# Attention and top-1 experts on one core: four wide warming products of TensorE give way to 53 small ones

## The chip, the cores and the metric

The program runs on one core of one Trainium2 chip. Its time is the device time of that core in microseconds (us); of the kernel before there are three timed runs, and one more execution was taken with the hardware profiler. Engines are named as the profile names them: PE (TensorE, its matrix products), PEld (TensorE's loads of the stationary operand), DVE (VectorE), ACT (ScalarE), POOL (GpSimd) and SP (SyncE, which here issues most of the transfers).

## The reference

Causal attention with a decay per head, in blocks, for 4 batches, 8 heads, 768 positions and 64 features, then a layer of 8 experts in which each of the 3072 tokens goes to one of them:

```python
intra = np.einsum('bhic,bhjc->bhij', qb, kb) * Dmask[None]       # Dmask = lam ** (i - j), i >= j
intra = np.einsum('bhij,bhjd->bhid', intra, vb)
inter = np.einsum('bhid,bhde->bhie', qb * lam_pow[None], kv_state)
out[:, :, sl] = intra + inter
kv_state = lam_block[None, :, None, None] * kv_state + np.einsum('bhsd,bhse->bhde', kb_dec, vb)
...
logits = x @ w_gate
expert_idx = np.argmax(logits, axis=1)
...
    h = np.maximum(xe @ w1[e], 0.0)
    out[mask] = gate_w[mask, None] * (h @ w2[e])
```

## The kernel before

The kernel has two stages. The attention stage walks over twelve steps (`order`: six blocks of 128 positions by two pairs of batches), in the loop over `i` at the end of the main function. In a step PE turns the keys and queries of the step ahead (`turn_k`, L353, into tiles `tk`; `turn_q`, L335, into `tq`), makes the routing logits of the step behind (`leave`, L480 and L485), applies the masked scores to the values (`attend_early`, L435, and `attend_late`, L443, into `op`), makes the scores of the step ahead (`score_half`, L389 and L394, into `sp`), ranks the tokens (`rank_of`, L560 and L562), applies the carried state (L421) and grows it (`grow`, L461, into `cp`). Nearly all of these are products of 64 or 128 rows by 64 or 128 columns. ACT and DVE empty the results from PSUM. SP issues the loads of queries, keys and values three steps ahead (L128), in rows of 256 bytes, and POOL issues two indirect writes per step (`send`, L541), which scatter the finished tokens to their experts' lists `xs`.

The expert stage (from about 127 us on) gathers the lists, and runs the two weight products of each expert; most of PE's time there is in L837, with 178 to 209 columns moving in each product.

The order of PE's instructions is the order in which the program is written, since the code stands in `tc.manual_schedule` for PE. All of PE's instructions, apart from a last part that runs only if an expert has too many tokens, are one straight stream without a loop.

The change is at the start. `run_up(count)` issues `count` bf16 products of a constant `ones` with itself (128 by 128 weights, 512 columns moving) into a spare bank; their results are not read. PE begins with `run_up(4)`, then `spread_lam` (L223), a product with one row, which spreads the eight decays `lam` over 128 partitions, and then a second `run_up(4)`. Behind it stand the first step's `turn_q` for its two halves (L335) with `run_up(2)` and `run_up(1)`, `turn_k` (L353) and the first scores (L389). DVE reads `spread_lam` (L225) and makes the decay tables from it.

A product of two fp32 operands is one line of the program and two pairs of instructions of PE in the trace, each a weight load and a product (L223 is one product in the program, and x2 in the trace); a transposition (L335, L353) and a bf16 product are one pair.

## Time and profile before

| | us |
|---|---|
| three timed runs: median (lowest to highest) | 441.4 (438.82 to 443.08) |
| the profiled execution: device time | 436.91 |
| its span, first to last instruction | 435.1 |
| PE busy in the span | 414.0 (95%) |
| PEld busy | 388.3 (89%) |
| DVE busy | 297.3 (68%) |
| ACT busy | 143.2 (33%) |
| POOL busy | 96.3 (22%) |

PE and PEld overlap, since the next weights are loaded while a product runs. The ends of products are modelled in the trace and their starts are not, so the pitch from start to start is the sharper measure. An idle time marked "issue" is one for which the trace shows no other engine or transfer that PE waited for.

### The profile page before, as it was taken

Reading aid. Unit: us, or ns where it says so; the run is one execution under the profiler, and the core shown is the slowest. Engines: PE = TensorE matmul, PEld = TensorE weight load, DVE = VectorE, ACT = ScalarE, POOL = GpSimd, SP = SyncE. Lnnn points to the kernel's source line nnn. Section 1 sums busy time; section 2 is a strip of 40 time slices with the busy share of each in tenths; the row PEclk is TensorE's granted clock in tenths of the full one; section 3 lists DMA queues with packets and bytes.
Section 4 is the critical chain, followed back from the end, with each engine's and each line's share of the span. In section 5 each row is a group of like instructions: output and inputs, shape, how many; then the busy total and the mean of one; then the engine's idle time right before and its main releaser. Section 6 shows DMA issues by size and latency. Waiting matters only on the chain.

```text
span 435.1 us, 11634 instructions
## 1 busy us (share of the span) xinstructions
PE 414.0 (95%) x4721; PEld 388.3 (89%) x4721; DVE 297.3 (68%) x692; ACT 143.2 (33%) x301; POOL 96.3 (22%) x123
## 2 busy tenths in 40 slices
PE   8988888999989999999999999999999999999993
PEld 5887777898878899999999999999999999999672
DVE  6777776588756876767669577766967867775601
ACT  3544344344432121330252135025214313403420
POOL 7545444441142210010011003001100200300502
PEclk9999999899999999999999999999999999999997
DMA  9988999899971499695399179638917946605201
GB/s 211 212 207 228 241 240 228 203 262 241 235 297 52 129 333 383 144 342 143 84 303 298 24 176 328 196 82 271 327 42 210 350 97 167 241 2 144 63 28 56
DMA packets 124784, 85.05 MB, mean 195 GB/s; under 512 B 83830, under 2 KB 106118, under 8 KB 124722
## 3 DMA queue, kind: packets, MB, share of 16 engines
q1 hardware_dynamic: 118720, 70.21, 59.5%
q0 software_dynamic: 4432, 13.61, 8.5%
q8 instruction: 39, 0.64, 0.6%
q10 hardware_dynamic: 1570, 0.39, 0.4%
q14 instruction: 23, 0.19, 0.1%
HBM read 65.10 MB, written 19.42 MB: 194 GB/s over the span
## 4 chain that ended last, share of the span: by engine, by line
PE 94%; issue 3%; DVE 1%; ACT 1%; POOLq 0%; POOL 0%; ACTq 0%
PE p L837 55%; PE p L945 6%; PE ph L724 5%; PE op L443 3%; PE cp L461 3%; PE op L421 3%; PE tk L353 3%; PE sp L389 3%; PE tq L335 3%; PE tx L480 2%; PE po L894 2%; PE logits L485 2%; PE op L435 2%; PE po L989 2%; PE sp L394 1%
## 5 line engine op out<-in xcount | busy, mean ns | idle before, releaser
L689 POOL DMA_INDIRECT out_dram<-o,ids x13 | 12.9, 989 | 171.0 <-ACT o L936 168.9
L837 PE MATMUL p<-hT,w2t 128*128 128x209 f32 (+5 forms) x288 | 49.4, 327 | 0.0
L837 PEld LDWEIGHTS p<-hT,w2t 128*128 128x128 f32 x288 | 47.7, 189 | 0.0
L765 ACT COPY u_qsT<-p 128x418 f32<-128x418 f32 (+6 forms) x40 | 19.2, 480 | 78.0 <-PE p L837 76.7
L541 POOL DMA_INDIRECT xs<-x,row x24 | 23.8, 991 | 74.8 <-ACT xT L451 31.7
L837 PE MATMUL p<-xgT,w1t 128*128 128x209 f32 (+6 forms) x224 | 38.7, 326 | 0.0
L837 PEld LDWEIGHTS p<-xgT,w1t 128*128 128x128 f32 x224 | 36.7, 190 | 0.0
L862 ACT ACTIVATE hT<-hT 128x418 f32<-128x418 f32 (+6 forms) x42 | 22.0, 525 | 32.5 <-DVE hT L861 32.5
L404 DVE TENSOR_TENSOR mt<-sp,tables 128x384 f32<-128x384 f32 x48 | 24.2, 549 | 7.8 <-PE sp L394 7.7
L451 ACT COPY xT<-op 128x512 f32<-128x512 f32 x24 | 12.9, 589 | 39.2 <-PE op L421 38.2
L861 DVE TENSOR_TENSOR hT<-p,u_qsT 128x418 f32<-128x418 f32 (+6 forms) x28 | 15.6, 558 | 11.9 <-ACT u_qsT L765 9.2
L724 PE MATMUL ph<-xgT,w1t 128*128 128x256 f32 (+1 forms) x128 | 21.9, 329 | 0.0
L750 DVE TENSOR_TENSOR u_qsT<-p,u_qsT 128x418 f32<-128x418 f32 (+6 forms) x20 | 11.2, 559 | 15.7 <-PE p L837 15.7
L913 DVE STREAM_TRANSPOSE yb<-yT 128x896 f32<-128x896 f32 (+2 forms) x14 | 13.6, 975 | 11.4 <-ACT yT L880 9.0
L724 PEld LDWEIGHTS ph<-xgT,w1t 128*128 128x128 f32 x128 | 19.2, 190 | 1.8 <-DVE gates_0a L634 0.2
L837 PE MATMUL p<-t_xT,s_q 128*128 128x209 f32 (+6 forms) x112 | 20.6, 326 | 0.0
L837 PE MATMUL p<-t_kd,w1t 128*128 128x209 f32 (+6 forms) x112 | 20.5, 326 | 0.0
L837 PE MATMUL p<-t_sd,w1t 128*128 128x209 f32 (+6 forms) x112 | 20.5, 326 | 0.0
L837 PE MATMUL p<-xgT,s_v 128*128 128x209 f32 (+6 forms) x112 | 20.5, 326 | 0.0
L837 PE MATMUL p<-xgT,s_k 128*128 128x209 f32 (+6 forms) x112 | 20.5, 326 | 0.0
L345 DVE TENSOR_TENSOR qsT<-tq,qdec 128x512 f32<-128x512 f32 x20 | 12.9, 685 | 9.4 <-ACT qT L341 9.4
L355 ACT COPY kT<-tk 128x512 f32<-128x512 f32 x24 | 14.3, 606 | 13.6 <-PE tk L353 13.5
(247 smaller groups left out, 920.3 us busy)
## 6 DMA issues: line engine op xcount, KB each, us to landing
w1t<-in_moe_w_dram SPq DMA_DIRECT2D x7, 2048.0 KB, 9.0
w2t<-in_moe_w_dram SPq DMA_DIRECT2D x7, 2048.0 KB, 9.8
qkv_in<-in_q_dram SPq DMA_DIRECT2D x12, 256.0 KB
q_in<-in_q_dram SPq DMA_DIRECT2D x12, 256.0 KB
y<-ye SPq DMA_DIRECT2D x6, 512.0 KB, 4.2
xb<-xs SPq DMA_DIRECT2D x32, 96.0 KB, 8.8
xb<-xs SPq DMA_DIRECT2D x24, 112.0 KB, 8.4
ye<-yb SPq DMA_DIRECT2D x12, 224.0 KB, 3.2
```

Source lines behind the costliest of these rows:

```text
L335: nc.tensor.transpose(tq[:, a, b], m.q[:, u, at:at + 2], ident)
L353: nc.tensor.transpose(tk[:, a, b], m.k[:, u, at:at + 2], ident)
L355: nc.scalar.copy(kT, tk)
L404: made = nc.vector.tensor_mul(mt[:, r], m.sp[a][r], decay[:, r, a].unsqueeze(1).to_broadcast(shp))
L541: put = tc.keep_in_program_order(nc.gpsimd.indirect_dma_start(out=xs, out_offset=bass.IndirectOffsetOnAxis(ap=row, axis=0), in_=src, in_of ...
L724: nc.tensor.matmul(ph, lhsT=piece(w1t, dc, fc), rhs=m.xgT[:, dc].rearrange("p k h -> p (k h)"), start=(dc == 0), stop=(dc == DC - 1))
L765: nc.scalar.copy(dst, src)
L837: nc.tensor.matmul(p[:, i, :], lhsT=lhs_of(lhs, rhs, c, i), rhs=rhs_of(lhs, rhs, c, i), start=(first and i == 0 and c == 0), stop=(c == ch ...
L861: nc.vector.tensor_add(outs[i][k], p, u)
L862: nc.scalar.activation(outs[i][k], outs[i][k], ACT.Relu)
L913: nc.vector.transpose(m.yb[:, i * nb:(i + 1) * nb], m.yT[i].rearrange("p d (b t) -> p b d t", t=Q))
L945: nc.tensor.matmul(p, lhsT=lhs[:, fc, :], rhs=rhs[:, fc, :], start=(first and fc == 0), stop=(fc == FC // 2 - 1), skip_group_check=True)
```

## The change

The second `run_up(4)` is replaced by `pace()`. It issues 53 products of the row `one` with itself: fp32, one row, 32 columns of weights (`Q` is 32), one column moving, all into the same 32 values of the spare bank (bank 7). Nothing reads them.

```diff
+    PACE = 53
+
+    def pace():
+
+
+        spare = bank(7, [Q, 1], "pace")
+        for j in range(PACE):
+            nc.tensor.matmul(spare, lhsT=one[:, :Q], rhs=one[:, :1], start=True, stop=True)
+
     with tc.manual_schedule(engines={mybir.EngineType.PE}):
         run_up(4)
         spread_lam = bank(6, [P, H], "lam")
         nc.tensor.matmul(spread_lam, lhsT=one, rhs=lam_row, start=True, stop=True)
-        run_up(4)
+        pace()
     nc.vector.tensor_copy(lam_bc, spread_lam)
```

PE's order of before, from the product that spreads the decays (`lam`) to the first transpositions of queries (`tq`); `spare` are the products of `run_up`:

```order
L223 MATMUL lam<-lam_row,one 128x8
L217 LDWEIGHTS ones
L217 MATMUL spare<-ones 128x512
L217 LDWEIGHTS ones
L217 MATMUL spare<-ones 128x512
L217 LDWEIGHTS ones
L217 MATMUL spare<-ones 128x512
L217 LDWEIGHTS ones
L217 MATMUL spare<-ones 128x512
L335 MATMUL tq<-impulse,qkv_in 128x128 x4
```

The same place of the changed kernel, in which all lines behind the new function stand 9 further on (L344 is the L335 of before):

```order
L232 MATMUL lam<-lam_row,one 128x8
L227 MATMUL pace<-one 32x1 x53
L344 MATMUL tq<-impulse,qkv_in 128x128 x4
L217 LDWEIGHTS ones
L217 MATMUL spare<-ones 128x512
```

Four pairs of a weight load and a product, 8 instructions, have gone. 53 fp32 products have come, which at two pairs each are 212 instructions. So every later instruction of PE stands 204 places further on in PE's stream, and none changes its place against another.

The second place is the end of a step and the beginning of the next, the same in both kernels but for the numbers of the lines; here as it stands before. `cp` is the growth of the state, `tk` and `tq` the turned keys and queries of the next step:

```order
L421 MATMUL op_2182<-qsT,st 64x128
L461 MATMUL cp<-qkv_in,kd 64x64 x16
L353 MATMUL tk<-impulse,k_in 128x128 x4
L335 MATMUL tq<-impulse,q_in 128x128 x8
L353 MATMUL tk<-impulse,k_in 128x128 x4
L480 MATMUL tx_2376<-impulse,xT 128x128 x4
```

Nothing moved there against its neighbours. What differs is the count of instructions from the start of the stream to this place, by 204. On the other engines the order is unchanged.

## Rows read from the trace of the kernel before

**Rows 1.** The page: busy time, share of the span and instructions of each engine
```profile
PE 414.0 (95%) x4721; PEld 388.3 (89%) x4721; DVE 297.3 (68%) x692; ACT 143.2 (33%) x301; POOL 96.3 (22%) x123
```

**Rows 2.** The page: the chain that ended last, by engine
```profile
PE 94%; issue 3%; DVE 1%; ACT 1%; POOLq 0%; POOL 0%; ACTq 0%
```

**Rows 3.** PE's waits in the whole span: total us, times, longest us
```profile
PE op L443 <- issue: 6.0, 5, 2.0
PE cp L461 <- issue: 2.8, 5, 1.1
PE op L421 <- issue: 1.5, 1, 1.5
...
PE op L421 <- DVE mt L404: 0.8, 1, 0.8
```

**Rows 4.** PE in order of time: start, length, products, idle before
```profile
105.42 1.15 PE L443 MATMUL op<-mt,v_in 128*64 128x64 f32 x32
106.50 0.67 PE L389 MATMUL sp<-qT,kT 64*64 64x128 f32 x16
```

**Rows 5.** PE in order of time, the same place of an earlier step
```profile
52.69 0.80 PE L443 MATMUL op<-mt,v_in 128*64 128x64 f32 x20
54.38 0.57 PE L443 MATMUL op<-mt,v_in 128*64 128x64 f32 x12 [0.89 <-issue]
54.87 0.67 PE L389 MATMUL sp<-qT,kT 64*64 64x128 f32 x16
...
58.48 0.74 PE L461 MATMUL cp<-v_in,kd 128*64 128x64 f32 x17 [0.23 <-issue]
...
59.64 1.04 PE L335 MATMUL tq<-impulse,q_in 128*128 128x128 f32 x8
```

**Rows 6.** Stretches: length, then busy time and instructions by engine, clock, DMA share, GB/s
```profile
54.38:65.61 11.23, 9.32 (x252) 8.32 (x253) 8.82 (x35) 4.49 (x11) 5.00 (x5) 1.00 0.97 239
...
77.12:87.50 10.38, 10.38 (x253) 9.44 (x254) 6.02 (x18) 4.36 (x10) 5.00 (x5) 0.84 0.88 223
87.50:96.34 8.84, 8.84 (x259) 8.12 (x256) 7.05 (x25) 4.20 (x10) 4.14 (x5) 1.00 1.08 260
```

**Rows 7.** The page: the DMA queue of instructions: packets, MB, share of 16 engines
```profile
q8 instruction: 39, 0.64, 0.6%
```

**Rows 8.** DMA queues at work from 58.48 to 63.2 us, all of them
```profile
q1 hardware_dynamic: 3694, 0.93, 86.8%
q0 software_dynamic: 84, 0.29, 16.0%
```

**Rows 9.** DMA queues at work from 63.2 to 63.8 us
```profile
q0 software_dynamic: 45, 0.19, 79.5%
...
q8 instruction: 1, 0.02, 9.7%
```

**Rows 10.** PE in order of time, three more ends of "issue" waits
```profile
65.61 0.57 PE L443 MATMUL op<-mt,v_in 128*64 128x64 f32 x12 [1.68 <-issue]
...
69.72 0.74 PE L461 MATMUL cp<-v_in,kd 128*64 128x64 f32 x17 [0.23 <-issue]
...
77.12 0.57 PE L443 MATMUL op<-mt,v_in 128*64 128x64 f32 x12 [1.95 <-issue]
```

**Rows 11.** PE in order of time at the start
```profile
2.89 0.59 PE L223 MATMUL lam<-lam_row,one 1*128 1x8 f32 x2
3.42 1.89 PE L217 MATMUL spare<-ones 128*128 128x512 bf16 x4
5.09 1.06 PE L335 MATMUL tq<-impulse,qkv_in 128*128 128x128 f32 x4
...
6.80 0.65 PE L335 MATMUL tq<-impulse,qkv_in 128*128 128x128 f32 x4
```

**Rows 12.** PE in order of time at 153 us, products with few columns moving
```profile
153.25 0.66 PE L712 MATMUL tr<-impulse,xg 65*128 65x65 f32 x8
153.75 0.43 PE L945 MATMUL p<-t_v,hT 128*128 128x256 f32 x1
```

## Prediction

> **What bounds the kernel now.** I read the page first. PE is busy in 95% of the span [rows 1], and the chain that ended last is 94% PE and 3% "issue" [rows 2]. Whatever moves PE's time in a stretch therefore moves the end nearly one for one, and the 3% of "issue" (some 13 us) is time in which PE waited for nothing that the trace shows.

> Next I read PE's waits. Its largest are just these "issue" waits: 6.0, 2.8 and 1.5 us, 10.3 us together in 11 places, all in L443, L461 and L421, lines of the attention stage. No transfer of data stands among PE's waits, and the next largest, for another engine, is 0.8 us [rows 3].

> The third view is PE in order of time. In an undisturbed step a run of 32 products of L443 takes 1.08 us, from its start at 105.42 to the start of L389 at 106.50 [rows 4]. In the step at 52.69 it breaks off behind the 20th product, goes on at 54.38, and L389 starts at 54.87, 2.18 us behind the run's start [rows 5]. So this stall costs 1.10 us where its idle column says 0.89, and the 10.3 us of idle time stand for about 10.3 x 1.10 / 0.89 = 12.7 us of loss.

> When is a block fetched? From the border at 58.48 on there is no q8 packet until 63.2, and within this time POOL's scatter (queue q0) sets in [rows 8]; one lies in 63.2 to 63.8, where q0 takes 79.5% [rows 9], and PE goes on at 65.61 [rows 10]: 7.1 us from border to border. From 54.38 to 58.48 it is 4.1 us [rows 5]. Had several blocks been fetched ahead, neither would stall. So one block is asked for when the one before it is entered; it is there after some 4 us, or after 6 to 7 when the scatter is on the way, and PE needs 8.84 us for two blocks where nothing stalls [rows 6].

> **The change, part by part.** *Removed: four wide products.* They run from 3.42 to 5.09, where the first transpositions of queries start [rows 11]: 1.7 us of PE on a path that is PE's own.

> *Added: 53 products, 106 pairs.* The trace has no such pair. Low end: from 153.25 to 153.75 eight pairs with 128 columns of weights and 65 moving start, 62 ns each, at the full clock [rows 12]; a quarter of the weights at half the clock is 62 / 4 x 2 = 31 ns, so 106 x 0.031 = 3.3 us. High end: the two pairs of `lam`, with one row as well, take from 2.89 to 3.42, 265 ns each [rows 11], which would be 28.1 us; but they wait for a semaphore, are waited for, and are no stream. A stream is nearer to rows 12; I take 45 ns, 4.8 us. Net of the removal PE is 3.1 us later (1.6 to 26.4).

> [...]

> *The clock.* [...] `pace` moves one column by one row. [...] I take 1.2 us (0 to 3).

> *Moved: every border.* All later instructions stand 204 further on, so a border falls 204 instructions earlier in the program or, modulo 256, 52 later: 26 pairs. The border in L443 (12 pairs left at 54.38) moves to the 14th product of L389, at about 55.3, and the one in L461 (17 left at 58.48) into L335, at about 60.0 [rows 5]. The small stall of 0.5 us lies between them, so that without it the first block is 4.7 - 0.5 = 4.2 us long and the second 8.84 - 4.2 = 4.6. Before, they are 4.1 - 0.5 = 3.6 and 8.84 - 3.6 = 5.2. So:

> - The fetches asked for in L443 come in about 4.1 us and miss 3.6; asked for in L389 they meet 4.2. Those stalls (L461, 2.8 us idle [rows 3]) go.
> - The fetches asked for in L461 are the long ones. Two of the five stalls behind them have both ends in rows: 7.1 us, and 7.4 from 69.72 to 77.12 [rows 10]. The other three have (6.0 - 1.68 - 1.95) / 3 = 0.8 us idle each [rows 3, 10], 1.0 of loss, so 6.2 us. In L335 they are asked for 1.5 us later. If the packet goes at the same moment as before, since it goes when what is on the way lets it, the waits are 4.7 (three), 5.6 and 5.9 against 4.6, and 2.6 us are left. If it takes as long as before from the asking, 10.1 us are left. The late packet went in the midst of the scatter and not behind it [rows 9], which is nearer to the first; I take 4 us.
> - The stall of 1.5 us in L421 [rows 3] stands alone, at the end of the stage; I count it as gone, as the wide products of the expert stage make the block there long.

> So 12.7 us become 4. One more effect: behind the longest stall, the 1.95 us before 77.12 [rows 10], the granted clock is 0.84 in the mean, and the step lasts 10.38 us with PE never idle, against 8.84 for the next [rows 6]. Without that stall the 1.5 us go too. In the expert stage no "issue" wait is listed [rows 3]; nothing changes there.

> *Sum against the profiled execution* (436.91 us: a span of 435.1 and 1.8 around it): -12.7 + 4.0 - 1.5 + 3.1 + 1.2 = -5.9, so 431.0. That execution is 4.5 us below the median of the three runs, and below all of them. I put the same difference on the median: 441.4 - 5.9 = **435.5 us**.

> **Rivals.**
> - *The stalls move along with the border.* The fetch takes as long from the asking as before: 441.4 - 12.7 + 10.1 - 1.5 + 4.3 = 441.6, no change. For it: the five long waits differ little (6.2 to 7.4). Against it: the fetches asked for in L443 take 4.1, so the wait depends on what else is on the way.
> - *The fetch is not the cause.* The stalls then stay where they are in the program, and only the start counts: 441.4 + 4.3 = 445.7. Against it stand the equal counts [rows 6, 10]. [...]
> - *Slower, by the price of the small products.* If each pair waits out the one before, as the two of `lam` may do, at 265 ns, the start is 26.4 us later: 441.4 - 12.7 + 4.0 - 1.5 + 26.4 + 1.2 = 458.8. It makes the kernel slower by over 1% from (4.4 + 12.7 - 4.0 + 1.5 - 1.2 + 1.7) / 106 = 0.143 us a pair on.
> - *Both borders meet the scatter.* If the fetches asked for in L389 also take 6.5 us, 13 us stand against 8.84 in each of six steps: 25 us of stalls, 441.4 - 12.7 + 25 - 1.5 + 4.3 = 456.5. Against it: L389 is half a step away from the scatter [rows 8, 9].

> **How the numbers follow.** Forecast 0.50 (its own range 430 to 440), stalls move along 0.20, fetch not the cause 0.10, dear small products 0.10, both borders 0.10. A measurement of this kernel can tell about 1% from no change: below 437.0 is faster, above 445.8 slower. Faster: 0.42 of the forecast and 0.05 of the first rival, 0.47. Same: 0.08 + 0.13 + 0.06 + 0.04 = 0.31, in the order of the cases. Slower: the rest, 0.22. The range of 429 to 447 leaves out the dear ends of the last two rivals; 429 is hardly any stall left, with pairs of 31 ns and no longer cold start.

> **What would show it.** In the changed profile: `pace` x106 in about 5 us; the "issue" waits of L443 and L461 gone and smaller ones, if any, in L389 and L335 (by the new numbers L398 and L344); steps of about 9 us from 27 us on; no low clock behind 77 us. The forecast is wrong if `pace` lasts over 15 us, or if PE's "issue" waits still add up to 8 us.

## The result and the profile after

The changed kernel takes 441.17 us (median of 20 runs, 438.88 to 445.08), the kernel before, run beside it, 440.01 (20 runs, 435.64 to 445.5). The ratio is 1.0061, 95% interval 1.0033 to 1.0088: slower by 0.6%, where 1.3% faster had been forecast. The ratio leaves out slow runs, those over 1.5% above the fastest of their kernel (four of before, none of the changed kernel); over all runs the means are 0.4% apart. The profiled execution has a span of 438.8 us against 435.1.

PE's waits in the changed kernel, in the columns of [rows 3]:

```profile
PE op L430 <- DVE mt L413: 2.4, 5, 0.6
PE sp L398 <- issue: 2.1, 3, 1.3
PE op L444 <- issue: 1.1, 3, 0.4
PE spare L217 <- DVE ones L155: 1.1, 1, 1.1
PE logits L494 <- issue: 1.0, 1, 1.0
PE tx L489 <- ACT xT L460: 0.7, 1, 0.7
...
PE op L452 <- issue: 0.2, 1, 0.2
```

The waits of [rows 3] in L443 and L461 (now L452 and L470) have gone but for 0.2 us, and "issue" adds up to 4.4 us in the place of 10.3. 3.1 us of it sit where the moved borders are, in L398 and at 126 us in L494; the 1.3 us in L444 and L452 are not at borders. New is the first row: L430 waits for DVE's mask `mt` five times, where before waited once.

PE in order of time at the start, to be laid beside [rows 11]:

```profile
3.42 5.81 PE L227 MATMUL pace<-one 1*32 1x1 f32 x106
9.16 1.12 PE L344 MATMUL tq<-impulse,qkv_in 128*128 128x128 f32 x4
```

And PE at the first sums of the expert stage, first before, then after:

```profile
146.34 1.89 PE L945 MATMUL p<-t_k,s_h 128*128 128x256 f32 x8
```

```profile
149.87 1.89 PE L954 MATMUL p<-t_k,s_h 128*128 128x256 f32 x8
```

These are 3.5 us apart, and from this place to the start of the last product both kernels need 281.0 us. The whole difference is made ahead of the expert stage. Starts of the same product in the two traces, laid side by side, are 5.6 us apart at 12 us, 0.2 at 84 us, and 3.5 again from 131 us on.

### The profile page after: what moved, and what is told of

The parts are those of the page before. It is cut to its first block, busy times and chain, and to the rows that moved or that the text cites. A ratio compares the mean times of both kernels' runs of the same rounds, so it can differ in the third digit from the quotient of the medians.

```text
span 438.8 us, 11838 instructions
## 1 busy us (share of the span) xinstructions
PE 421.2 (96%) x4823; PEld 395.1 (90%) x4823; DVE 298.2 (68%) x692; ACT 144.7 (33%) x301; POOL 96.1 (22%) x123
## 4 chain that ended last, share of the span: by engine, by line
PE 89%; DVE 6%; issue 2%; ACT 1%; POOLq 0%; POOL 0%; ACTq 0%
PE p L846 54%; PE p L954 5%; PE ph L733 5%; PE tk L362 3%; PE tq L344 3%; PE op L430 2%; PE cp L470 2%; PE tx L489 2%; DVE sh L509 2%; PE logits L494 2%; PE po L903 2%; PE po L998 2%; PE op L452 2%; PE sp L398 2%; PE pace L227 1%
## 5 line engine op out<-in xcount | busy, mean ns | idle before, releaser
L870 DVE TENSOR_TENSOR hT<-p,u_qsT 128x418 f32<-128x418 f32 (+6 forms) x28 | 15.6, 558 | 11.9 <-ACT u_qsT L774 9.2
L398 PE MATMUL sp<-qT,kT 64*64 64x128 f32 x384 | 20.1, 280 | 2.9 <-issue 2.1
L398 PEld LDWEIGHTS sp<-qT,kT 64*64 64x64 f32 x384 | 13.3, 135 | 6.3 <-issue 3.9
```

What stands on the lines that cost most here:

```text
L398: nc.tensor.matmul(sp[r][halves[u], b, u:u + 2], lhsT=m.kT[u][halves[r], a, b, halves[u]], rhs=m.qT[u][halves[r], a, b, :], start=(b == 0) ...
L870: nc.vector.tensor_add(outs[i][k], p, u)
```

## The experiments

Ratios are to the kernel before in the same series, with the 95% interval, which reaches 0.3 to 0.7% to either side; ratios of two series that lie less than about 0.6% apart are not told apart by it. A mark (+) or (-) shows what an edit puts in or takes out of the changed kernel, if no other is named.

### Does a stall belong to the border? (first series, before 441.2 us)

66 products put the borders back where before has them (+256 instructions):

```diff
-    PACE = 53
+    PACE = 66
```

> 66 small products in place of 53: 264 instructions come and 8 go, 256 net, so every border of a block of 256 falls on the same instruction as before, while the start is even longer. Border theory (a stall is PE waiting for its next 256 instructions, and the small products only move the borders): the start is 5.6 us later as in the changed kernel plus 26 pairs of 54 ns, 7.0 us in all; the issue waits are back in L443 and L461 (by the new numbers L452 and L470), about 9 to 12 us idle; time 440.0 + 7.0 = 447. Rival (the stalls depend on when things happen and not on which instruction stands at a border): the waits stay where the changed kernel has them, in L398, and the time is that of the changed kernel plus 1.4, 442.6.

446.89 us, ratio 1.018 (1.0116 to 1.0243). PE's waits in it:

```profile
PE op L452 <- issue: 7.5, 6, 2.0
PE cp L470 <- issue: 3.1, 3, 1.3
```

The stalls are back on the very lines of [rows 3], with 13 more products that nobody reads. That these waits belong to the borders of blocks of 256 instructions is shown: with 256 instructions more than before they are back (7.5 and 3.1 us), with 204 more 0.2 us of them is left, and with 128 more (below) they stand in L405. And in the changed kernel, from 69.83 to 89.23 us, the ends of two waits in L398, PE's records are 504 products, 504 loads and 16 waits for semaphores, 1024, which is four times 256. But this kernel is only 5.2 us slower than the changed one, 1.4 of it for 26 more pairs.

The same borders with the four wide products kept, the small ones over four column tiles (64 here, 51 in the kernel whose borders are those of the changed one):

```diff
-        spare = bank(7, [Q, 1], "pace")
+        spare = bank(7, [P, 1], "pace")
         for j in range(PACE):
-            nc.tensor.matmul(spare, lhsT=one[:, :Q], rhs=one[:, :1], start=True, stop=True)
+            at = slice(j % 4 * Q, (j % 4 + 1) * Q)
+            nc.tensor.matmul(spare[at], lhsT=one[:, :Q], rhs=one[:, :1], start=True, stop=True)
...
+        run_up(4)
         pace()
```

> As the kernel with the wide products kept and 51 small ones, with 64 small ones: 256 instructions come, so borders as in the kernel before, and a start within 0.4 us of the one with 51. The difference of the two is the worth of the border alone. Border theory: issue waits back in L443 and L461 (L454 and L472 here), 9 to 12 us idle, 440.0 + 1.9 = 442, 4 to 5 us above the one with 51. Rival (stalls do not follow the border): both the same within 1 us.

> The four wide products kept, and behind them 51 small ones over four tiles: 204 instructions come, the same borders as in the changed kernel. Expected: the clock rises near 7 us as in the kernel before, the start is about 1.5 us later than before (102 pairs at 14 ns), stalls as in the changed kernel; 440.0 + 1.5 - 4.4 = 437. If the pairs stay at 54 ns or 27 ns at the full clock: 3 to 5.5 us late, 438.5 to 441. If other engines bound the stage: 440 to 441.5.

With 64: 441.36 us, 1.0057 (1.0014 to 1.01). With 51: 439.29, 1.0007 (0.9962 to 1.0053). The shift of the borders alone is worth 2.1 us, half of what was expected, and the two intervals overlap.

### What does the start cost?

53 products over four column tiles, as above but without the wide products:

> The changed kernel with its 53 small products spread over four tiles of 32 columns, one behind the other, instead of all in one. Same number of instructions, same borders. The routing products L485 go over four such tiles at 14 ns a pair (32 pairs in 0.65 us), so 106 pairs would take 1.5 us instead of 5.8. Theory that the start eats what the borders give: tq starts near 5 us instead of 9.2, the low clock may still last to 7 or 10 us, so the start is 0 to 2 us late instead of 5.6 and the time is 441.2 - 4.1 = 437. Rival (the 54 ns are a floor of the single small product, whatever the tile): no change against the changed kernel, 441.2. Rival (another engine or the transfers bound the attention stage once PE's stalls go): the start is shorter but the time stays at 440 to 441.

```profile
3.42 1.65 PE L228 MATMUL pace<-one 1*32 1x1 f32 x106
5.00 1.12 PE L345 MATMUL tq<-impulse,qkv_in 128*128 128x128 f32 x4
```

438.98 us, 1.0014 (0.9979 to 1.0048). A pair falls from 54 to 15 ns, `tq` starts 4.2 us earlier than in the changed kernel, and the time falls by only 0.47%, 2.1 us. Starts of the same products in the two profiled executions show where the lead goes: it is 4.0 us at 31 us of the changed kernel, 2.3 at 106 and 1.6 at 134.

### Are the loads of w2t the late hold-up? (second series, before 437.5 us)

In the changed kernel PE trickles at 117 us (its products come in small groups with waits between), not at a border, while SP issues the loads of w2t:

```profile
116.04 0.90 PE L444 MATMUL op<-mt,v_in 64*64 64x64 f32 x26
117.33 0.36 PE L444 MATMUL op<-mt,v_in 64*64 64x64 f32 x5 [0.39 <-issue]
118.12 0.24 PE L444 MATMUL op<-mt,v_in 64*64 64x64 f32 x1 [0.43 <-issue]
```

So these loads were issued later, by ScalarE, in three kernels:

```diff
-                for g in range(DC):
-                    load_chunks(w2t, g)
                 weights.append((w1t, w2t))
...
+        for g in range(DC):
+            chunks = slice(g * FC // DC, (g + 1) * FC // DC)
+            nc.scalar.dma_start(out=weights[0][1][:, chunks], in_=w2_r[0][:, chunks])
         hidden(passes[0], w1t, range(2))
```

> The changed kernel, with one thing moved: the four loads of w2t (512 KB each) are issued by ScalarE after the attention loop, near 129 us, in the place of SP near 116 us; VectorE reads w2t first near 145 us. Theory: the hold-up of TensorE, VectorE and ScalarE between 116 and 119 us (L444 in trickles, 1.83 us; lg of L503 waits 2.2 us) comes from these loads, which lie on top of the scatters of GpSimd and the loads of w1t, so it goes: no idle time over 0.5 us on TensorE or VectorE there, and the time falls by 1.5 to 2.5 us, to about 439. Rival: the hold-up is that of the scatters or of something else and stays, or what it gives is waited for further on in the stage (ScalarE, VectorE, the last block of instructions): less than 0.7 us of gain, 441.

> The kernel before with the same move of the loads of w2t. Before has its hold-up a little later (2.27 us in L421 at 124.2, while a scatter of 1.21 us and a fetch of instructions run). Theory (the loads of w2t lengthen what else is in flight): gain of 1 to 2.5 us, 438 to 439. Rival (the loads have nothing to do with it): within 0.7 us of before.

> The kernel with four wide products kept and 51 small ones behind them over four column tiles (borders as in the changed kernel), with the loads of w2t moved to ScalarE at 129 us. With its loads on SP TensorE waits 3.2 us for xgT of ScalarE near 121 us. Theory: that wait shrinks below 1 us and the time is 436 to 437, under that of before. Rival: the wait stays or is paid further on, 439.

Changed kernel: 438.13 us, 1.0012 (0.9981 to 1.0042), half a per cent below the ratio without the move, which was measured in another series; of the trickle one wait of 0.3 us is left, and the products from 106 to 134 us of the changed kernel take 24.5 us in the place of 27.8. Before: 436.36, 0.998 (0.9949 to 1.0011), no difference that can be told. With 51 small products: 434.10, 0.9906 (0.9873 to 0.994), faster than both kernels. In the same series borders half way, 32 small products with the wide ones kept and the loads of w2t unmoved:

> Four wide products kept, 32 small ones behind them over four column tiles: 128 instructions more than before, half a block, so every border of a block lies half way between those of before and the changed kernel's side of it; loads of w2t as before. Theory (what a border costs is set by where it lies in the step of the attention loop): the issue waits sit on other lines than L443, L461 of before and L398 of the changed kernel, and their sum lies anywhere between 2 and 13 us, the time follows it at a third to a half, 438 to 443. Rival (the fetches have nothing to do with those waits): waits stay on the same products as in before and the time is 441 plus 0.5 for the small products.

434.24 us, 0.9936 (0.9899 to 0.9972), though PE's waits list

```profile
PE sp L405 <- issue: 6.8, 7, 2.0
```

6.8 us of stalls, 2.4 more than in the changed kernel, and 1.2% faster. Part of this is the cheaper start (`tq` at 5.6 us in the place of 9.2). But between the same two products of PE, at 31 and 106 us of the changed kernel, it takes 75.0 us against 74.6, with 6.3 us of "issue" waits against 1.7. Stalls of PE do not add up to time here: the first sign of what the later runs show. Single executions differ by as much as 2.1 us there: the same instructions take 78.8 us in before and 76.7 in before with late w2t, which differs only from 115 us on.

### Is it the scatters? (third series, before 441.7 us)

Every scatter of the attention stage is issued twice, the second time into an array that nobody reads, in the changed kernel and in the kernel before:

```diff
             spread(m.x[:, j], m.row[:, j:j + 1])
+            again = tc.keep_in_program_order(nc.gpsimd.indirect_dma_start(
+                out=xs2, out_offset=bass.IndirectOffsetOnAxis(ap=m.row[:, j:j + 1], axis=0),
+                in_=m.x[:, j], in_offset=None))
...
```

> The changed kernel with every scatter of the attention stage issued a second time by GpSimd into an array that nobody reads (256 rows of 2112 bytes a step more; GpSimd itself is busy 22 per cent). Theory: a block's fetch shares the 16 transfer engines with scatter and loads, so more traffic makes it later: median time from TensorE's entering a block to the end of the fetch up from about 3 us by 0.3 to 1 us, issue waits from 4.4 to 7 us or more, time up by 2 to 5 us. Rival: the fetch has a time of its own, whatever else is moved: issue waits stay within 1.5 us of 4.4 and the time within 1 us.

> The kernel before with every scatter of the attention stage issued a second time into an array that nobody reads. Theory (traffic makes the fetch later): issue waits at L443 and L461 up from 10.3 us by 2 us or more, time up by 1 to 5 us. Rival: within 1 us of before, issue waits within 1.5 us.

471.33 us, 1.0664 (1.0631 to 1.0696), and 465.27, 1.0542 (1.0488 to 1.0596): some 27 and 24 us more, about five times the most that was expected, and by neither theory. No "issue" wait over 1.2 us is left, and at a border none over 0.3; from PE's entering a block to the end of the next packet of q8 it takes 2.5 us in the median of 22 blocks, against 2.9 in the changed kernel. So here more scatter does not make the fetch later. What became longer is the step. POOL in order of time, in the changed kernel with doubled scatters (the copies are those of L600):

```profile
45.09 1.01 POOL L551 DMA_INDIRECT xs<-x,row  x1 [4.58 <-DVE mt L414]
46.40 0.96 POOL L600 DMA_INDIRECT xs<-x,row  x1 [0.30 <-issue]
47.67 0.96 POOL L551 DMA_INDIRECT xs<-x,row  x1 [0.30 <-issue]
48.93 0.96 POOL L600 DMA_INDIRECT xs<-x,row  x1 [0.30 <-issue]
...
57.44 1.01 POOL L551 DMA_INDIRECT xs<-x,row  x1 [4.50 <-ACT xT L461]
```

From step to step it is 12.35 us. The same engine in the changed kernel:

```profile
53.28 1.01 POOL L550 DMA_INDIRECT xs<-x,row  x1 [4.50 <-ACT xT L460]
54.59 0.96 POOL L550 DMA_INDIRECT xs<-x,row  x1 [0.30 <-PE tq L344]
55.58 1.05 POOL L388 TENSOR_TENSOR sd<-st,sdec 128x512 f32<-128x512 f32 x1
56.58 2.03 POOL L374 TENSOR_TENSOR kd<-k_in,kdec 128x512 f32<-128x512 f32 x2
63.09 1.01 POOL L550 DMA_INDIRECT xs<-x,row  x1 [4.48 <-ACT xT L460]
```

9.81 us, and 12.35 is 2.54 more: twice the 1.27 us from one scatter to the next. In the changed kernel the seven steps from 33 to 103 us last 9.96, 9.83, 9.81, 10.42, 9.82, 9.81 and 9.80 us; in before 9.95, 11.02, 9.93, 11.24, 11.88, 9.96 and 9.80. In all kernels with single scatters so far none of these seven steps is under 9.80. That is a floor, and PE does not set it: in 53.28 to 63.09 PE is busy for 9.34 us.

The floor is a loop, to be followed in DVE of the changed kernel, with PE, which hangs on it, in the second fence:

```profile
57.01 1.64 DVE L509 TENSOR_TENSOR sh<-lg,mx 128x16 f32<-128x16 f32 x1
58.69 0.18 DVE L512 SCALAR_TENSOR_TENSOR key<-sh,rev 128x16 f32<-128x16 f32 x1
...
60.15 1.00 DVE L413 TENSOR_TENSOR mt<-sp,tables 128x384 f32<-128x384 f32 x2
...
62.16 0.16 DVE L544 SCALAR_TENSOR_TENSOR row<-far,near 128x2 int32<-128x2 int32 x1
```

```profile
60.74 1.10 PE L430 MATMUL op<-qsT,st 64*64 64x128 f32 x32 [0.34 <-DVE mt L413]
```

Scatter, scatter, `sd` and `kd` end at 58.61 on POOL. `sh`, 16 numbers a partition and 0.17 us long at 106.72, ends 0.04 us later. In every kernel before the last series each `sh` of over 0.3 us ends within 0.05 us of the end of a piece of `kd`. Behind it come, without a wait on DVE, the rest of the routing, the mask and the places of the tokens up to `row`, which ends at 62.32, and 0.77 us later, at 63.09, the next scatter: 5.33 us on POOL, 0.04, 3.67 on DVE and 0.77 are the 9.81. The trace names ACT's `xT` as what POOL waited for, but releasers are inferred, and this one is wrong: in every kernel the first scatter of each of these steps sets in 0.77 to 0.80 us behind the end of `row` (0.90 in the first), while the last `xT` ended 0.06 us ahead of it here and 11.85 in before at 81.91, where the scatter does not wait for its step's own `xT`. So PE is no link of the loop; L430 only waits for its mask. Inside `kd`, `mx`, with one input, takes 0.17 us at 56.81, and `sh`, with two, 1.64 us at 57.01; why `sh` lasts until `kd` ends is not shown.

### Why four scatters in a row, at 117 us?

Two more kernels of the third series had the loads of w2t late:

> Four wide products kept, 32 small ones over four column tiles (128 instructions more than before), and the loads of w2t issued by ScalarE at 129 us. Theory: the two gains lie in different stretches (borders up to 115 us, transfers behind it) and add: with 32 small products alone the ratio to before was 0.994, and the move of the loads was worth 0.2 to 1.0 per cent in the other three kernels, so 0.984 to 0.992. Rival: the stretch from 113 to 128 us was already free with 32 small products (its only waits there are 0.3 and 0.9 us), so the move gives nothing: 0.993 to 0.995.

> The changed kernel with both costs taken out: its 53 small products lie over four column tiles (1.7 us for all in the place of 5.8), and the loads of w2t are issued by ScalarE at 129 us. Theory: without the late hold-up (3 us of trickle near 121 us in the kernel with column tiles alone) the ratio to before falls from 1.0014 to 0.990 to 0.994. Rival: the hold-up has another cause here, 0.998 to 1.002.

439.06 us, 0.9938 (0.9896 to 0.998), and 438.73, 0.9953 (0.992 to 0.9986). The hold-up is there without the loads of w2t. In the second:

```profile
116.87 0.96 POOL L551 DMA_INDIRECT xs<-x,row  x1 [15.34 <-DVE place L587]
118.14 0.96 POOL L551 DMA_INDIRECT xs<-x,row  x1 [0.30 <-issue]
119.40 1.08 POOL L551 DMA_INDIRECT xs<-x,row  x1 [0.30 <-issue]
120.79 0.96 POOL L551 DMA_INDIRECT xs<-x,row  x1 [0.31 <-issue]
```

```profile
120.36 1.12 PE L490 MATMUL tx<-impulse,xT 128*128 128x128 f32 x4 [3.05 <-issue]
```

POOL waits 15 us and then sends two steps' scatters at once. PE's wait of 3.05 us is one for ACT's `xT`, which sets in at 119.72 us, 2.4 us behind the end of the product that it reads, for no reason that the trace names. POOL waits for the rows `xg`, which are read out of the array that the scatters write: in all kernels with single scatters the first one comes 1.3 to 2.5 us behind the last packet of `xg` (115.1 us here). So in a last but one series (before 438.75 us) the first half of w1t was loaded behind `xg`:

```diff
-            if FIRST_W1 <= i < FIRST_W1 + 2:
-                for d in range(2 * (i - FIRST_W1), 2 * (i - FIRST_W1) + 2):
+            if i == FIRST_W1 + 1:
+                for d in range(DC):
```

> 53 small products over four column tiles, loads of w2t on ScalarE at 129 us, and now the first eight loads of w1t (128 KB each) issued behind the load of xg in the place of ahead of it. Theory: the load of xg lands late behind other loads (its last packet near 115 us), the scatter of the next step may only start 1.8 us after that, four scatters then go in a row (116.9 to 121.8 us) and hold TensorE up by 3.3 us; with xg landing earlier there is one pair at 110 to 114 us and one behind it, no gap over 1.3 us on TensorE between 112 and 126 us, and the ratio to before falls from 0.995 to about 0.988. Rival: the late loads are not what delays xg, or the hold-up comes whatever the scatters do: 0.995.

> The kernel with 32 small products and late loads of w2t, and the same move of the loads of w1t. There xg's last packet is at 120.7 us and four scatters go in a row from 122.5 us. Theory: xg lands below 115 us, scatters go in pairs, waits of tx for ScalarE's xT (2.5 us) go, ratio from 0.994 to about 0.988. Rival: 0.994.

> The kernel with 51 small products and late loads of w2t, and the same move of the loads of w1t. There xg already lands at 113.1 us and the scatters go in pairs. Theory: nothing to gain, ratio 0.988 to 0.993 as without the move (0.9906). Rival (fewer loads between 101 and 111 us speed up the steps in any case): 0.985 or less.

435.20 us, 0.9933 (0.9897 to 0.997); 434.89, 0.9927 (0.9891 to 0.9963); 434.91, 0.9908 (0.9872 to 0.9944). In the first `xg` lands at 111.3 us, the scatters go in pairs (112.87, 114.13, 119.02), and the longest idle time of PE there falls from 3.1 to 0.7 us. In the second `xg` still lands at 116.1 and four go in a row, yet PE, DVE and ACT make no pause together. So four in a row follow a late `xg`; that they bring the hold-up is not shown, and in the ratios its end is worth 0.2%, less than the intervals. Why the engines pause in some kernels stays open.

### Is the loop the floor? (last series, before 440.1 us)

The second scatter is issued behind `kd`, in before, in the changed kernel and in the one with 51 small products and late w2t:

```diff
-    def send(m):
-        for j in range(2):
-            spread(m.x[:, j], m.row[:, j:j + 1])
+    held = []
+
+    def send(m, hold=False):
+        spread(m.x[:, 0], m.row[:, 0:1])
+        held.append(m)
+        if m.last_early or not hold:
+            send_rest()
...
+    def send_rest():
+        while held:
+            m = held.pop()
+            spread(m.x[:, 1], m.row[:, 1:2])
...
                 decay_k(ahead)
+            send_rest()
...
-                send(last)
+                send(last, True)
```

> The kernel before, with GpSimd's second scatter of each attention step issued behind sd and kd of that step in the place of ahead of them (1.27 us less between the first scatter and kd). Theory: from 28 to 102 us a step cannot be shorter than 9.81 us, because a loop runs round it: first scatter, second scatter, sd, kd on GpSimd (5.3 us), then sh, the routing chain and the mask on VectorE (sh ends when kd ends), L421 and xT, and again the scatter; TensorE's border stalls partly lie beside it. With 1.27 us less in the loop it is 8.5 us, and TensorE's own work (9.2 to 9.5 us a step) and its border stalls set the step: 9.3 to 9.5 us where no stall falls, steps with stalls 0.5 to 1.3 us shorter than now (11.0 to 11.9), 2 to 5 us over the stage, ratio 0.988 to 0.996. Rival: sh's long time ends with kd by chance and TensorE alone sets the step: no step under 9.7 us, ratio 0.998 to 1.003.

> The changed kernel with the same move of the second scatter. Theory: its steps of 9.81 us are the loop's own (five of seven are 9.80 to 9.83), so it gains more than the kernel before does: steps of 9.2 to 9.5 us, 3 to 5 us over the stage, ratio 0.994 to 0.999 in the place of 1.006; sh takes 0.2 to 0.5 us in the place of 1.5. Rival: steps stay at 9.8 us and the ratio at 1.006.

> The kernel with 51 small products over four column tiles behind the four wide ones and late loads of w2t (ratio 0.9906), with the same move of the second scatter. Theory: its steps of 9.81 us fall to 9.2 to 9.5, ratio 0.981 to 0.986. Rival: steps stay at 9.8 us, ratio 0.9906.

442.76 us, 1.0128 (1.0062 to 1.0193); 439.77, 1.0027 (0.9985 to 1.0069); 437.14, 0.9974 (0.993 to 1.0017). The mechanism came, the gain did not: in the changed kernel the ratio is 0.3% lower, which the intervals don't part from nothing, in before there is a loss, and the third is slower than without the split by 0.7%, over two series whose intervals overlap a little. The third has four scatters in a row again, from 116.2 us, and PE waits 4.8 us there. In before with the split, DVE, then POOL, then PE:

```profile
74.93 0.21 DVE L500 TENSOR_TENSOR sh<-lg,mx 128x16 f32<-128x16 f32 x1
```

```profile
71.08 0.96 POOL L541 DMA_INDIRECT xs<-x,row  x1 [4.06 <-ACT xT L451]
...
80.17 0.96 POOL L541 DMA_INDIRECT xs<-x,row  x1 [3.90 <-ACT xT L451]
```

```profile
43.59 0.57 PE L443 MATMUL op<-mt,qkv_in 128*64 128x64 f32 x12 [1.76 <-issue]
48.52 0.74 PE L461 MATMUL cp<-qkv_in,kd 128*64 128x64 f32 x17 [1.05 <-issue]
55.99 0.83 PE L443 MATMUL op<-mt,v_in 128*64 128x64 f32 x12 [2.02 <-issue]
```

`sh` is short again and a step of 9.09 us appears, under the floor, as do steps of 8.92 in the second kernel and 8.81 in the third: the loop is shown. But the same run takes 12.4 us from 43.59 to 55.99, with two stalls. What takes the gain back stands in PE's waits from 33 to 103 us, in the changed kernel without and with the split:

```profile
PE op L430 <- DVE mt L413: 2.4, 5, 0.6
PE sp L398 <- issue: 1.5, 2, 1.3
```

```profile
PE tq L344 <- issue: 2.2, 5, 1.0
PE op L452 <- issue: 1.7, 5, 0.4
PE sp L398 <- issue: 1.1, 3, 0.5
PE op L444 <- issue: 0.4, 1, 0.4
```

The waits for the mask are gone, and "issue" waits have come: in L344 and L398 at the borders, and in L444 and L452 away from them; these six each end 1.3 to 1.4 us behind the start of the second scatter, and their cause stays open. The seven steps take 71.7 us in the place of 69.4. So the loop is a floor, and taking it away alone gains nothing.

## Why the prediction was wrong

**What bounds the kernel** is the step that failed. "Whatever moves PE's time in a stretch moves the end nearly one for one" was read from PE's busy share and from an undisturbed step of 8.84 us. In the attention stage none of the seven steps goes under 9.80 us in any kernel with both scatters ahead of `kd`, wherever PE stalls, because of the loop through POOL and DVE. [Rows 6] show 8.84 us from L443 to L443, a place that can lie early or late within the loop; POOL's own steps there are 9.96 and 9.80 us. With 9.34 us of work in 9.81, PE has about half a microsecond a step to spare (an estimate), and what falls into it costs nothing. For the seven steps, 73.8 us in before, the forecast's terms make about 67 us (an estimate); the floor is 68.6, and the changed kernel needs 69.4.

The loop is not the whole miss. Forecast and traces are 9.4 us apart: 1.3 at the start, 3.7 in the attention stage up to 106 us, and 4.4 behind it. There the prediction had only stalls that go, and put new ones at nothing; in the trace L398 and L494 stall at borders (0.9 and 1.2 us), and L444 and L452 trickle (1.8), for a cause that stays open.

**The sum, term by term**, by starts of the same products in the two profiled executions, one of each kernel:

| term | predicted, us | measured, us |
|---|---|---|
| start: `pace` for the wide products | +3.1 | +4.07 |
| start: slower pace of the products lasts longer | +1.2 | +1.53 |
| stalls at the old borders | -12.7 | -12.4 |
| stalls at the new borders | +4.0 | +5.8 |
| low clock behind 77 us (0.84 before, 1.00 after) | -1.5 | -0.9 |
| L430 waits for DVE's mask | none | +1.9 |
| trickles in L444 and L452 at 37 and 117 us | none | +2.4 |
| the rest, many small pieces | none | +1.1 |
| sum | -5.9 | +3.5 |

- **The borders** were right: block, place, which stalls go (all five of L461, the five of L443, and that of L421 with 1.71 us) and where new ones come (one in L344, seven in L398, one in L494).
- **The stalls left** were 5.8 and not 4, within the bounds 2.6 and 10.1. The fetches asked for in L344 are the late ones, as said: from PE's entering the block to the end of the next packet of q8 it takes 3.0 to 4.8 us for the nine blocks that begin there, and 2.4 to 3.1 for the eight that begin in L398. Their stall shows a border on, in L398.
- **The premise of that step** was wrong: the late packet was put down to the scatter on the way. With twice the scatters the fetch is no later (2.5 us in the median, against 2.9). When an instruction packet goes out stays open.
- **The start** was 5.6 and not 4.3: a pair of `pace` takes 54 ns, where 45 was taken (over four column tiles it takes 15), and the products behind it keep a slower pace for longer: eight `tk` take 1.91 us at 12.20, where before has 1.04 at 7.51. No run shows where the 1.2 us come from that the sum has for the clock; what the two traces show in their place is 1.53 us of such products.
- **What no term had**: in before the stall in L443 lies ahead of the scores, and DVE's routing with the long `sh` goes on beside it, so that the mask is nearly ready when PE comes. Take the stall away, and PE comes to L430 earlier and waits for the mask. The long `sh` was in the trace of before (1.55 us at 52.68, 0.17 at 105.42), in DVE's rows, which the prediction did not read. PE's waits of before, too, hold one more than [rows 3] show: 1.1 us for DVE's `ones` at the very start, so 0.8 us is not the largest wait for another engine.
- **The rivals**: "the fetch is not the cause" falls with 66 products. "The stalls move along" came closest in time (441.6), but for another reason: half of the stalls did go, and the start, the waits for the mask and the trickles took back what they gave. The dear small products fall with 54 ns a pair, "both borders" with 5.8 us of stalls where it had 25. The forecast's own tests held ("issue" below 8 us, `pace` in 5.8 us, no low clock behind 77 us: 1.00 from 77 to 90), except for "steps of about 9 us".

## What to carry to other kernels

Before a stall of the busiest engine is counted as gain, follow one step of the loop round all engines, from an instruction to the same one a step later: if the shortest steps all have the same length (here 9.80 to 9.83 us), a loop through another engine may be the floor, and only what stands above it can be had. An instruction that takes ten times its usual time on another engine (here `sh`, 1.64 us in the place of 0.17) can mark such a loop. Which instruction releases a wait is told by a distance that is the same in every step (here 0.77 to 0.80 us), more surely than by the name that the trace gives. And a floor that is taken away can give nothing, where other waits take its place (here 1.0061 and 1.0027). Nor need stalls at the borders show in the time: the kernel with 6.8 us of them, at 434.24 us, was among the fastest.

## What was not expected of the hardware

- A pair of 32 columns of weights and one column moving, one row, takes 54 ns in one tile (at 3.4 to 9.2 us of the changed kernel), and 15 ns when four column tiles take turns (at 3.4 to 5.0 us).
- The same first products reach their quicker pace at different times: eight `tk` take 1.91 us at 12.20 in the changed kernel, and 1.07 at 13.58 in the one with 66 small products.
- POOL needs 1.27 us from one scatter to the next in a row, and with two scatters more in each step the step went from 9.81 to 12.35 us.
- Behind several scatters in a row PE, DVE and ACT can pause together, with no wait that the trace could name: for 2.6 us from 121.6 us in the kernel with 51 small products. In the one with 32 and late loads of w1t and w2t, also with four in a row, they don't.
